# A recurrent attention, a dense MLP and a routed MLP on one core: the first gather of rows issued ahead of weight loads, more identity matmuls on TensorE, small routing results in PSUM

## The chip, the core and the metric

The kernel runs on one core of one Trainium2 chip. The metric is device time in microseconds, from one execution to the next the same program on the same data. The engines are named as the profile names them: PE is TensorE's matmul and PEld its weight load, DVE is VectorE, ACT is ScalarE, POOL is GpSimd, SP is SyncE, whose queue issues most of the DMAs. PE, DVE, ACT, POOL and SP each take their own instructions in the order of the program and wait on semaphores for one another.

## What is computed

Three stages follow each other, all in float32. The attention is a linear recurrence over 768 steps for 4 x 8 heads of size 48; its output is laid out as 3072 tokens of 384. A dense MLP with a leaky activation follows, then a gate with 8 columns, and a greedy assignment that takes the logits in falling order and fills each of 8 experts with exactly 384 tokens. Each expert is a two-layer MLP on its own tokens.

```python
for t in range(S):                                   # S = 768, per batch and head
    y[:, :, t] = rt . (state + u*kt (x) vt)
    state = w * state + kt (x) vt
h = x @ w_in; x = (max(h, 0) + alpha * min(h, 0)) @ w_out   # 3072 x 384 -> 2048 -> 384
for idx in argsort(-logits.flatten()):               # logits = x @ w_gate, 3072 x 8
    if assigned[tok] >= 0 or counts[e] >= cap: continue     # cap = 384
    assigned[tok] = e; counts[e] += 1
out[mask] = max(x[mask] @ w1[e], 0) @ w2[e]          # w1: 384 x 1024, w2: 1024 x 384
```

## The kernel before

**Setup and attention.** The recurrence is done in 24 chunks of 128 steps (4 batches by 6). `att_setup` builds powers of w by doubling on DVE and POOL (`PW`, `IW`, `TK`, `TR`), issues the first loads of k, r and v on SP, and prepares the first two chunks. Per chunk, `scale_k` multiplies k by powers of w (on POOL unless an engine is handed over), `turn_k` transposes the product on PE, `keep_k` copies the transposed tile to SBUF on ACT (`KT`), `scale_r` scales r on DVE (`RT`), `product` multiplies `RT` by `KT` (`prod`, on POOL unless handed over), and `sums` multiplies `prod` by `uw` on PE with two columns at a time, where `uw` is u times w. `keep_sums` copies the result (`cs`) on DVE. `scores` (`pA`) and the rest of `turn(i)` follow. In line 271, `warm(n)` issues n matmuls of the identity with itself on PE, whose result nobody reads; one appears in the trace as two instructions. The list `WARM` holds how many stand at each place of the setup: 8, 8 and 4, and a fourth entry that nothing uses. Beside the chunks, float64 words of the MLP's weights are taken apart on DVE (lines 481 to 488, `ti` and `tf`) and split into a high and a low part on ACT and POOL (lines 491, 492).

**Dense MLP.** Seven groups of tokens run with PE as the busy engine; every factor is split into a high and a low float32r part, so each product is three matmuls. The rows are written to `md` in DRAM by SP (line 650). In the last group the second layer is put off (`rest`), and its matmuls are spread over the steps of the first routing.

**Routing.** `route(p)` picks the tokens of the p-th expert to be filled. `close(p)` narrows a threshold in four passes: DVE compares (`G`, line 839), PE counts with six matmuls against one-hot rows `ohr` (`cnt`, line 844), and DVE transposes, sums and updates (`tr`, `tot`, `Je`, `jt`, `fl`, lines 848 to 859). After the fourth pass DVE finds the expert number (`F`, `Jm`, `sel`, `es`, `ei`, lines 861 to 874) and the members (`memb`). `lists` and `compact` turn members into row numbers (`px`, `ip`, `iw`, `idx`). `next_picks` and `next_ones` take the members out and prepare the keys and the one-hot rows (`eq`, `S`, `ohr`, which ACT copies three times, line 767) of the next pass. `tot` and the second `jt` are tiles in SBUF; `S` is one PSUM tile in which most other small results of the routing lie.

**First routing and first gather.** `first_route` runs `route(0)` beside `rest`. As soon as `ei` is known, `wload` issues the first expert's weights on SP: eight pieces of 384 KB into eight `raw` buffers, w1 in pieces 0 to 3 and w2 in 4 to 7. The first four go out at once; with `PRE` = 1 one of them is split in the same stretch (`wsplit`: a cast on ACT, line 1135, and a subtraction on POOL, line 1136). The other four wait, since POOL writes one element of each of their buffers (line 1125), and that stands behind the gather in POOL's queue. The last tile of the dense MLP is copied by ACT (line 649) and written to `md` by SP (line 650), behind the first four loads. `gather` then issues three indirect DMAs on POOL (line 1142), 128 rows each.

**Experts.** The string `START` sets the order of the work around the gather, a letter each: `d` takes the remaining loads, `c` is one step of the second routing, `t` transposes one of the three gathered tiles on PE (line 1156), `l` makes its low part on DVE (`fxl`), `w` splits one weight piece. `PLAN0` places the splits that are left. In the loop, `layer1` (line 1172, `eph`) and `layer2` (line 1189, `o`) of expert p share PE with one step of the routing of the next expert each (`step`), so that routing p+1 runs beside expert p.

Of the kernel before, what the change touches and what calls it, by code (L numbers as in the profile page):

```python
# [8 lines left out]
F32 = mybir.dt.float32  # L9
# [3 lines left out]
U32 = mybir.dt.uint32  # L13
# [5 lines left out]
P = 128  # L19
B, H, S, D = 4, 8, 768, 48  # L20
# [16 lines left out]
NP = 8  # L37
# [3 lines left out]
START = "dcccwtwltclwtlc"  # L41
# [3 lines left out]
WARM = (8, 8, 4, 4)  # L45
PRE = 1
BASE = 6
EXTRA = ()
PLAN0 = ((0, 0), (0, 1), (1, 0), (1, 1))
# [36 lines left out]
class Kernel:  # L86
# [29 lines left out]
    def route_consts(self):  # L116
# [31 lines left out]
        self.iot, self.jt = S[:, 168:192], S[:, 192:224]  # L148
# [5 lines left out]
    def att_setup(self, ctx):  # L154
# [41 lines left out]
        for i in range(8):  # L196
            if i < 7:
                v.reciprocal(IW[:, i, :], PW[:, i, :])
                v.tensor_mul(PW[:, i + 1, :], PW[:, i, :], PW[:, i, :])
            if i == 0:  # L200
                g.tensor_copy(TR[:, :, 127], IW[:, 0, :])
            else:
                i -= 1
                n = 1 << i
                pb = PW[:, i, :].unsqueeze(2).to_broadcast([112, 4, n])
                ib = IW[:, i, :].unsqueeze(2).to_broadcast([112, 4, n])
                v.tensor_mul(TK[:, :, P - 2 * n:P - n], TK[:, :, P - n:], pb)
                g.tensor_mul(TR[:, :, P - 2 * n:P - n], TR[:, :, P - n:], ib)
        TKm = ap.tile([P, 4, P], F32, name="TKm")
# [16 lines left out]
        for q in range(2):  # L226
            o = slice(64 * q, 64 * q + D)
            v.tensor_mul(self.uw[o, :, q], uc[o], PW[o, 0, :])
        self.keep_k(0)
        self.product(0, v)  # L230
        self.turn_k(1, tag="y", bufs=2)
        self.keep_k(1)
        self.sums(self.prod.pop(0))
        self.keep_sums(0)
        self.scale_k(2)
# [374 lines left out]
    def mlp(self, ctx):  # L610
# [41 lines left out]
        for gi, T in enumerate(GROUPS):  # L652
# [22 lines left out]
            for f in range(NF):  # L675
                if (gi, f) == (late - 2, 12):
                    self.route_consts()
                if gi == 0 and f == 8:
                    nc.sync.dma_start(self.wgb, bass.AP(tensor=self.w_gate.tensor, offset=self.w_gate.offset,
                                                        ap=[[0, P], [1, DM * E]]).rearrange("p (e c) -> p e c", e=E))  # L680
# [145 lines left out]
    def close(self, p):  # L826
# [5 lines left out]
        for s in range(STEPS):  # L832
# [16 lines left out]
            tot = rp.tile([P, E], F32, name="tot")  # L849
# [15 lines left out]
        jt = rp.tile([P, 32], F32, name="jt")  # L865
# [245 lines left out]
    def wload(self, ei, s, behind=False):  # L1111
# [4 lines left out]
        for c in range(NP):  # L1116
            raw = (self.rw if c < NP // 2 else self.rw2).tile([P, 2 * DM], F32, name="raw")
            if c < NP // 2:
# [4 lines left out]
            else:  # L1123
                if behind:
                    nc.gpsimd.memset(raw[:1, :1], 0.0)
# [7 lines left out]
    def wsplit(self, piece):  # L1133
        d, to = piece
        self.nc.scalar.copy(to[0], d)  # L1135
        self.nc.gpsimd.tensor_sub(to[1], d, to[0].bitcast(F32))  # L1136

# [81 lines left out]
    def route(self, p):  # L1219
# [7 lines left out]
        yield from cut(ls, 2 if p else 99)  # L1227
        if p < E - 1:
            self.next_picks(p)
        if p > 1:  # L1230
            yield
        yield from ls
        self.idxs[p] = self.idx
        if p < E - 1:
            self.next_ones(p)

    def first_route(self, rest):
# [4 lines left out]
        for n, _ in enumerate(self.route(0)):  # L1242
            if load is None and self.eis:
                load = self.load = self.wload(self.eis.pop(0), 0, True)
                self.pieces = [next(load) for _ in range(NP // 2)]
            elif len(self.pieces) > NP // 2 - PRE and n > 10:
                self.wsplit(self.pieces.pop(0))
            drain(cut(rest, REST[n]))

    def experts(self):  # L1250
# [18 lines left out]
        for c in START:  # L1269
# [8 lines left out]
            elif c == "w":  # L1278
                self.wsplit(self.pieces.pop(0))
            else:  # L1280
                self.pieces.extend(self.load)
# [121 lines left out]
```

## Time and profile before

| | us |
|---|---|
| median of 3 runs | 802.99 |
| lowest and highest run | 801.01, 804.59 |
| the profiled execution | 804.11 |
| its span from first to last instruction | 802.3 |
| PE busy in it | 769.6 |
| DVE busy in it | 589.3 |
| ACT busy in it | 409.6 |
| POOL busy in it | 279.5 |

A row of a timeline gives the start in microseconds from the span's start, the duration, engine, source line, operation, output and inputs, shapes and how many instructions were merged; the bracket at the end tells how long the engine stood idle before and what released it. [...] Times of the sections below are positions in this profiled execution.

### The profile page before, as it was taken

How to read it: one execution, taken by the hardware profiler on the slowest of the kernel's cores; microseconds unless marked ns; L12 is line 12 of the kernel's file. 1: busy time of each engine (PE TensorE's matmuls, PEld its weight loads, DVE VectorE, ACT ScalarE, POOL GpSimd, SP SyncE). 2: the span in 40 equal slices, each digit the busy share in tenths (PEclk: the TensorE clock that was granted, in tenths of full speed). 3: DMA queues.
4: the chain of work that ended last, by engine and by line, in shares of the span. 5: the costliest groups of instructions: out<-in, count | busy, mean ns of one | idle time of the engine just before them, and what ended most of it. 6: DMA issues, size and time to landing. Idle time of an engine off the chain costs nothing.

```text
span 802.3 us, 15416 instructions
## 1 busy us (share of the span) xinstructions
PE 769.6 (96%) x5539; PEld 706.0 (88%) x5539; DVE 589.3 (73%) x1601; ACT 409.6 (51%) x884; POOL 279.5 (35%) x273
## 2 busy tenths in 40 slices
PE   7999999999999999999999999995999999999996
PEld 6888987989999899999998999884889989889996
DVE  6899996997899999888885444776777778664220
ACT  3889896665444444534444455714335444344441
POOL 6788872322000000000000000006667766658661
PEclk8799999999999999999999999996999999999998
DMA  8688873620100200301020010014542553554300
GB/s 236 187 244 241 262 227 91 211 85 24 56 1 0 80 1 3 106 20 31 24 76 0 1 60 1 21 53 155 187 155 81 199 177 96 162 159 148 129 31 32
DMA packets 64579, 81.30 MB, mean 101 GB/s; under 512 B 8048, under 2 KB 55408, under 8 KB 64368
## 3 DMA queue, kind: packets, MB, share of 16 engines
q1 hardware_dynamic: 61008, 70.81, 28.5%
q0 software_dynamic: 3072, 9.44, 3.5%
q8 instruction: 45, 0.74, 0.4%
q14 instruction: 38, 0.31, 0.1%
q10 hardware_dynamic: 416, 0.00, 0.0%
HBM read 66.07 MB, written 14.16 MB: 100 GB/s over the span
## 4 chain that ended last, share of the span: by engine, by line
PE 69%; DVE 7%; issue 3%; ACT 2%; POOL 1%; DMA 1%; POOLq 0%; SPq 0%; another core or an unknown queue 0%; ACTq 0%; DVEq 0%
PE m L638 25%; PE ph L691 24%; PE eph L1172 9%; PE o L1189 9%; PE cnt L844 1%; DVE G L839 1%; PE ept L1156 1%; DVE gh L706 1%; POOL wbl L1136 1%; POOL out_dram L1198 1%; DVE fxl L1162 1%; ACT nt L695 1%; PE ip L949 1%; DMA xg<-md,idx 0%; DVE F L861 0%
## 5 line engine op out<-in xcount | busy, mean ns | idle before, releaser
L691 PE MATMUL ph<-xh,wah 128*128 128x512 f32 (+1 forms) x336 | 121.8, 363 | 1.0 <-ACTq L244 0.7
L691 PE MATMUL ph<-xh,wal 128*128 128x512 f32 (+1 forms) x336 | 121.5, 362 | 0.0
L691 PE MATMUL ph<-xl,wah 128*128 128x512 f32 (+1 forms) x336 | 121.5, 362 | 0.0
L695 ACT ACTIVATE nt<-ph 128x512 f32<-128x512 f32 (+1 forms) x112 | 60.2, 538 | 118.1 <-PE ph L691 112.1
L638 PE MATMUL m<-wbh,gl 128*128 128x384 f32 (+1 forms) x352 | 119.2, 339 | 0.4 <-DVE gl L717 0.4
L638 PE MATMUL m<-wbh,gh 128*128 128x384 f32 (+1 forms) x352 | 119.2, 339 | 0.0
L638 PE MATMUL m<-wbl,gh 128*128 128x384 f32 (+1 forms) x352 | 119.1, 338 | 0.0
L706 DVE SCALAR_TENSOR_TENSOR gt<-nt,al,gt 128x512 f32<-128x512 f32 (+1 forms) x96 | 67.8, 706 | 49.6 <-ACT gt L696 49.6
L714 ACT CAST gh<-gt 128x512 fp32r<-128x512 f32 (+1 forms) x96 | 56.3, 587 | 72.9 <-DVE gt L706 72.9
L1175 ACT ACTIVATE hh<-eph 128x384 fp32r<-128x384 f32 x64 | 31.5, 492 | 117.1 <-PE eph L1172 110.2
L134 POOL MEMSET io<- 128x1 f32 x1 | 0.1, 100 | 252.5 <-DVE io L133 252.5
L1180 DVE SCALAR_TENSOR_TENSOR hl<-eph,hh 128x384 fp32r<-128x384 f32 x64 | 35.5, 555 | 64.0 <-ACT hh L1175 57.6
L562 DVE SCALAR_TENSOR_TENSOR junk<-wt,wgb 128x384 f32<-128x384 f32 x128 | 71.3, 557 | 3.9
L691 PEld LDWEIGHTS ph<-xh,wal 128*128 128x128 f32 x336 | 63.1, 188 | 10.6
L691 PEld LDWEIGHTS ph<-xh,wah 128*128 128x128 f32 x336 | 63.1, 188 | 9.1 <-ACTq L244 1.0
L717 DVE TENSOR_TENSOR gl<-gt,gh 128x512 fp32r<-128x512 f32 (+1 forms) x96 | 61.8, 643 | 12.7 <-ACT gh L714 12.6
L1136 POOL TENSOR_TENSOR wbl<-raw,wbh 128x768 fp32r<-128x768 f32 x32 | 58.7, 1853 | 31.7 <-ACT wbh L1135 31.6
L691 PEld LDWEIGHTS ph<-xl,wah 128*128 128x128 f32 x336 | 63.1, 188 | 7.3
L1136 POOL TENSOR_TENSOR wal<-raw,wah 128x768 fp32r<-128x768 f32 x32 | 58.6, 1851 | 30.7 <-ACT wah L1135 27.9
L638 PEld LDWEIGHTS m<-wbh,gh 128*128 128x128 f32 x352 | 66.1, 188 | 3.4
L638 PEld LDWEIGHTS m<-wbl,gh 128*128 128x128 f32 x352 | 66.1, 188 | 3.3
L638 PEld LDWEIGHTS m<-wbh,gl 128*128 128x128 f32 x352 | 66.1, 188 | 0.7 <-DVE gl L717 0.7
(263 smaller groups left out, 1798.7 us busy)
## 6 DMA issues: line engine op xcount, KB each, us to landing
raw<-in_moe_w_dram SPq DMA_DIRECT2D x64, 384.0 KB
raw<-in_moe_w_in_dram SPq DMA_DIRECT2D x16, 384.0 KB
raw<-in_moe_w_out_dram SPq DMA_DIRECT2D x16, 384.0 KB
raw_r<-in_rt_dram SPq DMA_DIRECT2D x24, 224.0 KB
raw_k<-in_kc_dram SPq DMA_DIRECT2D x24, 192.0 KB
raw_v<-in_vc_dram SPq DMA_DIRECT2D x24, 192.0 KB
xd<-ysb SPq DMA_DIRECT2D x48, 96.0 KB
md<-raw SPq DMA_DIRECT2D x22, 192.0 KB
```

The lines of the kernel that those rows point to most:

```text
L562: v.scalar_tensor_tensor(junk, t, 1.0, self.wgb[:, e], op0=ALU.mult, op1=ALU.mult, accum_out=wc[:, f, e:e + 1])
L638: nc.tensor.matmul(acc[t][:, :N], a[:, o], self.wb[b][:, f, :N], start=(f == 0 and n == 0), stop=(f == NF - 1 and n == 2))
L691: nc.tensor.matmul(ph[:, :T], self.wa[a][:, k, fs], b[:, k, :T], start=(n == 0), stop=(n == 8))
L695: nc.scalar.activation(nt[:, :T], ph[:, :T], AF.Relu, scale=-1.0)
L706: v.scalar_tensor_tensor(gt[:, :T], nt[:, :T], self.al[:, f:f + 1], gt[:, :T], op0=ALU.mult, op1=ALU.add)
L714: nc.scalar.copy(h, g)
L717: v.tensor_sub(l, g, h.bitcast(F32))
L1136: self.nc.gpsimd.tensor_sub(to[1], d, to[0].bitcast(F32))
L1172: self.nc.tensor.matmul(ph, w1[a][:, k, f * P:(f + 1) * P], x[b][:, k], start=(n == 0), stop=(n == 8))
L1175: self.nc.scalar.activation(hh, ph, AF.Relu)
L1180: self.nc.vector.scalar_tensor_tensor(hl, ph, 0.0, hh.bitcast(F32), op0=ALU.max, op1=ALU.subtract)
L1189: self.nc.tensor.matmul(self.acc[q], h[a][:, o], w2[b][:, f], start=(f == 0 and n == 0), stop=(f == NS - 1 and n == 2))
```

## The change

Constants: `WARM` goes from (8, 8, 4, 4) to (8, 8, 10, 6), and its fourth entry is now used, between the transposes of the first two chunks and `sums`. `PRE` goes from 1 to 2. `START` and `PLAN0` are new; a digit n in `START` issues n identity matmuls, `s` does only the subtraction of a piece that was cast before.

```diff
-START = "dcccwtwltclwtlc"
+START = "dssc996ctc6tl6tlclc"
-WARM = (8, 8, 4, 4)
-PRE = 1
+WARM = (8, 8, 10, 6)
+PRE = 2
-PLAN0 = ((0, 0), (0, 1), (1, 0), (1, 1))
+PLAN0 = ((0, 0), (0, 1), (1, 0), (1, 1), (2, 0), (2, 1))
@@ att_setup
+        for q in range(2):                       # behind the loop that builds TR
+            o = slice(64 * q, 64 * q + D)
+            g.tensor_mul(self.uw[o, :, q], uc[o], PW[o, 0, :])
         self.scale_r(1)
-        for q in range(2):
-            o = slice(64 * q, 64 * q + D)
-            v.tensor_mul(self.uw[o, :, q], uc[o], PW[o, 0, :])
         self.keep_k(0)
         self.product(0, v)
+        self.scale_k(2, v)
         self.turn_k(1, tag="y", bufs=2)
         self.keep_k(1)
+        self.warm(WARM[3])
         self.sums(self.prod.pop(0))
         self.keep_sums(0)
-        self.scale_k(2)
         self.product(1)
@@ mlp, last group, f == 6
+                    i0 = self.rp.tile([2, 1], U32, name="i0")
+                    nc.gpsimd.memset(i0, 0)
+                    nc.gpsimd.indirect_dma_start(
+                        out=self.rp.tile([2, DM], F32, name="r0"), out_offset=None, in_=self.md[:P, :],
+                        in_offset=bass.IndirectOffsetOnAxis(ap=i0, axis=0))
@@ route_consts and close
-        self.iot, self.jt = S[:, 168:192], S[:, 192:224]
+        self.iot, self.jt, self.jt2, self.tot = S[:, 168:192], S[:, 192:224], S[:, 224:256], S[:, 256:264]
-            tot = rp.tile([P, E], F32, name="tot")
+            tot = self.tot
-        jt = rp.tile([P, 32], F32, name="jt")
+        jt = self.jt2
@@ wload: pieces in a given order; only the piece number `held` is written by POOL first
-        for c in range(NP):
+        for n, c in enumerate(order):
+            if n == held:
+                nc.gpsimd.memset(raw[:1, :1], 0.0)
-                if behind:
-                    nc.gpsimd.memset(raw[:1, :1], 0.0)
@@ first_route
-                load = self.load = self.wload(self.eis.pop(0), 0, True)
-                self.pieces = [next(load) for _ in range(NP // 2)]
-            elif len(self.pieces) > NP // 2 - PRE and n > 10:
-                self.wsplit(self.pieces.pop(0))
+                load = self.load = self.wload(self.eis.pop(0), 0, ORDER, PRE)
+                self.pieces = [next(load) for _ in range(PRE)]
+            elif 11 < n < 12 + PRE:
+                self.wcast(self.pieces[n - 12])
@@ route(p), p > 0: next_ones one step earlier
         if p > 1:
             yield
+        if p:
+            next(ls)
+        if p < E - 1:
+            self.next_ones(p)
+        if p:
+            yield
         yield from ls
-        if p < E - 1:
-            self.next_ones(p)
```

Two weight pieces now go out ahead of the gather instead of four, in the order 0, 1, 4, 2, 5, 3, 6, 7 (`ORDER`), and the third holds the five behind it on SP. Both early pieces are cast on ACT after the copy of the dense MLP's last tile, and their subtractions on POOL stand behind the gather.

On PE the setup reads as follows; `pt` and `pk` are transposes, `kvc` on the `uw` row is `sums`. Before:

```order
L212 MATMUL pt<-ident,TK 128x112 x4
L271 MATMUL warm<-ident 128x128 x4
L364 MATMUL pk<-ident,raw_p_116 112x128 x4
L364 MATMUL pk<-ident,raw_p_118 112x128 x4
L336 MATMUL kvc<-uw,prod 64x2 x8
```

Now:

```order
L215 MATMUL pt<-ident,TK 128x112 x4
L272 MATMUL warm<-ident 128x128 x10
L365 MATMUL pk<-ident,raw_p_116 112x128 x4
L365 MATMUL pk<-ident,raw_p_118 112x128 x4
L272 MATMUL warm<-ident 128x128 x6
L337 MATMUL kvc<-uw,prod 64x2 x8
```

Six more identity matmuls stand ahead of the first transposes, and six new ones between the transposes and the first `sums`.

On POOL, around the first gather (`xg` are the three gathered tiles, `wal` low parts of weights, `raw` the one-element write that lets later loads start, `r` the new small gather of two rows). Before:

```order
L141 MEMSET F 128x32
L796 COPY L<-M 128x176
L796 COPY L<-M 128x16
L1136 TENSOR_TENSOR wal<-raw,wah 128x3x256
L1142 DMA xg_6929<-md,idx 128x384
L1142 DMA xg_6931<-md,idx 128x384
L1142 DMA xg_6933<-md,idx 128x384
L1125 MEMSET raw 1x1 x4
```

Now:

```order
L141 MEMSET F 128x32
L681 MEMSET i_6421 2x1
L682 DMA r_6423<-md,i_6421 2x384
L803 COPY L<-M 128x176
L803 COPY L<-M 128x16
L1156 DMA xg_6937<-md,idx 128x384
L1156 DMA xg_6939<-md,idx 128x384
L1156 DMA xg_6941<-md,idx 128x384
L1126 MEMSET raw 1x1
L1146 TENSOR_TENSOR wal<-raw,wah 128x3x256 x2
```

The subtraction has moved behind the gather, and a small indirect DMA from `md` stands ahead of it, in the last group of the MLP.

On PE behind the first routing's last matmul (`iw`), where `o` are the transposes of the gathered tiles. Before:

```order
L957 MATMUL iw<-is__6880,two 32x6 x4
L844 LDWEIGHTS ohr_5665
L844 MATMUL cnt<-G,ohr_5665 128x128
...
L1156 MATMUL o_6971<-ident,xg_6929 128x128 x3
L1156 MATMUL o_6979<-ident,xg_6931 128x128 x3
```

Now:

```order
L964 MATMUL iw<-is__6887,two 32x6 x4
L272 MATMUL eph<-ident 128x128 x24
L851 LDWEIGHTS ohr_5678
L851 MATMUL cnt<-G,ohr_5678 128x128
...
L1170 MATMUL o_6994<-ident,xg_6937 128x128 x3
L272 MATMUL eph<-ident 128x128 x6
L1170 MATMUL o_7018<-ident,xg_6939 128x128 x3
L272 MATMUL eph<-ident 128x128 x6
L1170 MATMUL o_7031<-ident,xg_6941 128x128 x3
```

The 24 identity matmuls stand ahead of the second routing's first count and of the first gathered tile; the third transpose has moved ahead of the second count.

## Rows read from the trace of the kernel before

**Rows 1.** The granted clock in the page's 40 equal slices (20 us each), in tenths.

```profile
PEclk8799999999999999999999999996999999999998
```

**Rows 2.** Stretches: length; busy PE, PEld, DVE, ACT, POOL (instructions); PEclk, DMA share, GB/s.

```profile
16.00:29.00 13.00, 13.00 (x152) 11.33 (x152) 8.59 (x20) 9.52 (x27) 8.10 (x8) 0.50 0.79 214
30.00:43.00 13.00, 12.45 (x222) 10.81 (x218) 12.56 (x28) 12.06 (x36) 10.22 (x11) 1.00 0.71 176
```

**Rows 3.** Timeline of the setup: identity matmuls, uw, the two products, sums.

```profile
1.68 3.68 PE L271 MATMUL warm<-ident 128*128 128x128 f32 x16 [1.68 <-DVE ident L110]
...
8.17 1.07 PE L271 MATMUL warm<-ident 128*128 128x128 f32 x8
...
10.91 1.01 DVE L228 TENSOR_TENSOR uw<-uc,PW 48x4 f32<-48x4 f32 x2
...
11.87 1.26 POOL L376 TENSOR_TENSOR prod<-RT,KT 112x512 f32<-112x512 f32 x1 [0.15 <-ACT KT L370]
11.95 1.73 DVE L376 TENSOR_TENSOR prod<-RT,KT 112x512 f32<-112x512 f32 x1
...
13.73 0.63 PE L336 MATMUL kvc<-uw,prod 112*64 112x2 f32 x16 [2.62 <-DVE prod L376]
```

**Rows 4.** The chain that ended last, around the first gather: start, us, what.

```profile
537.71 3.25 DMA raw<-in_moe_w_dram
540.98 0.83 ACT wah L1135
541.81 0.39 ACT gt L649
542.21 2.77 DMA md<-gt
...
545.37 0.63 issue
...
546.22 3.88 DMA xg<-md,idx
550.15 0.92 PE o L1156 x3
...
553.85 3.26 PE eph L1172 x9
...
560.70 0.52 PE cnt L844 x6
```

**Rows 5.** Timeline of POOL and PE around the first gather.

```profile
542.56 0.24 PE L957 MATMUL iw<-is__6880,two 64*32 64x6 f32 x8 [0.55 <-DVE is__6880 L954]
...
546.22 1.15 POOL L1142 DMA_INDIRECT xg<-md,idx  x1 [2.52 <-DVE ohr L764]
...
546.51 0.80 PE L844 MATMUL cnt<-G,ohr 128*128 128x128 bf16 x6 [3.71 <-DVE G L839]
...
547.68 0.97 POOL L1142 DMA_INDIRECT xg<-md,idx  x1 [0.30 <-issue]
```

**Rows 6.** Timelines of later routings: F alone and beside POOL's subtraction, and PE's waits.

```profile
588.48 0.17 DVE L861 TENSOR_SCALAR F<-tot 128x8 f32<-128x8 f32 x1
...
645.55 5.44 POOL L1136 TENSOR_TENSOR wbl<-raw,wbh 128x768 fp32r<-128x768 f32 x3 [2.77 <-ACT wbh L1135]
...
645.84 1.61 DVE L861 TENSOR_SCALAR F<-tot 128x8 f32<-128x8 f32 x1
...
648.41 0.23 DVE L868 TENSOR_SCALAR S<-jt,Jm 128x8 f32<-128x8 f32 x1
...
650.35 0.19 PE L922 MATMUL px<-memb,tri 128*128 128x24 bf16 x1 [1.38 <-DVE memb L884]
...
703.32 1.84 POOL L1136 TENSOR_TENSOR wbl<-raw,wbh 128x768 fp32r<-128x768 f32 x1 [0.78 <-ACT wbh L1135]
...
703.61 1.58 DVE L861 TENSOR_SCALAR F<-tot 128x8 f32<-128x8 f32 x1
...
707.37 0.55 PE L1156 MATMUL ept<-ident,xg 128*128 128x128 f32 x3 [1.89 <-DVE fxl L1162]
```

**Rows 7.** A stretch behind that last wait, columns as in rows 2.

```profile
708.30:711.60 3.30, 3.30 (x13) 2.99 (x12) 2.25 (x9) 1.59 (x3) 2.36 (x2) 0.50 0.83 239
```

**Rows 8.** Timeline of PE: the first count of a later routing.

```profile
690.21 0.50 PE L844 MATMUL cnt<-G,ohr 128*128 128x128 bf16 x6 [0.88 <-DVE G L839]
```

More of the change, by code (lines that the diff above doesn't have):

```diff
@@ L677, in mlp @@
                     self.route_consts()
+                if (gi, f) == (late, 6):
+                    i0 = self.rp.tile([2, 1], U32, name="i0")
[3 more added lines that the diff above has]
+                        in_offset=bass.IndirectOffsetOnAxis(ap=i0, axis=0))
                 if gi == 0 and f == 8:
@@ L1109, in wset, with wload @@
                 [t[:, 3 * F2:].rearrange("p (f c) -> p f c", c=DM) for t in (h, l)])
-    def wload(self, ei, s, behind=False):
+    def wload(self, ei, s, order=range(NP), held=None):
         nc = self.nc
@@ L1131, in wload, with wcast, wsub, wsplit @@
             yield d, to
-    def wsplit(self, piece):
+    def wcast(self, piece):
         d, to = piece
         self.nc.scalar.copy(to[0], d)
+    def wsub(self, piece):
+        d, to = piece
         self.nc.gpsimd.tensor_sub(to[1], d, to[0].bitcast(F32))
+    def wsplit(self, piece):
+        self.wcast(piece)
+        self.wsub(piece)
     def gather(self, idx):
@@ L1227, in route @@
         yield from cut(ls, 2 if p else 99)
+        if not p:
+            self.idxs[p] = self.idx
         if p < E - 1:
@@ L1277, in experts @@
                 self.warm(int(c), self.ph.tile([P, CAP], F32, name="eph")[:, :P])
-            elif c == "w":
-                self.wsplit(self.pieces.pop(0))
+            elif c == "s":
+                self.wsub(self.pieces.pop(0))
             else:
```

## Prediction, made before the changed kernel ran

> **What bounds the kernel now.** I read the page's slices first. PE is busy nearly everywhere, so the places that matter are those where it waits or runs slowly, and the granted clock names them: it is down in the first two slices, in one near 550 us and in the last [rows 1]. [...] The timeline shows what PE did before the clock fell: it stood idle for 2.62 us until DVE's product was there [rows 3]. Around the gather I read the chain that ended last. It runs from a weight load over a weight cast on ACT, the copy of the MLP's last tile, its write to DRAM, and the gather, to the first layer-1 block of expert 0 at 553.85 [rows 4]. Behind it PE is again the bound, but for a few waits, which the later routings cause [rows 6, 8].
>
> **Setup: the first product.** `uw` moves from DVE to POOL, whose place for it is idle time. On DVE its two small operations took 1.01 us, since POOL was at work on k then, and DVE's product took 1.73 us with POOL's at 1.26 beside it [rows 3]. Where POOL started first, such a DVE operation ends only after it. Now DVE's product can start as soon as `KT` is there, before POOL's second product, and take some 0.7 us. Against that stand the ten identity matmuls ahead of the transposes. At the lower level one instruction takes 3.68 / 16 = 0.23 us; half of that, 0.115, is the price at full clock, near the 1.07 / 8 = 0.13 of the later block [rows 3]. So the block of 20 instructions lasts 2.3 us from 8.17 and holds the transposes back by some 0.4 us. `scale_k(2)` now stands on DVE between the product and `cs`, next to POOL's product, for 0.9 to 1.6 us. I take a gain of 0.4 us for all of this, out of 0 to 1.0 (the stretch in which DVE's product was held).
>
> **Setup: the clock.** The identity matmuls fill most of PE's gap: 2.3 us and then 12 x 0.115 = 1.4 us behind the transposes, so the idle time ahead of `sums` falls from 2.62 us to under 1. If the clock then stays up, DVE's idle time from 16 to 29, 13 - 8.59 = 4.4 us, falls towards the 13 - 12.56 = 0.4 of the later stretch [rows 2]. That is 4.0 us at the most. I take 3.4, since the first chunks have fewer matmuls to hide waits. The time carries through, as DVE works through its list in order until the dense MLP starts. If the clock falls as before, the gain is 0. Setup together: -3.8 us, from -0.4 to -5.0.
>
> [...] Between 8.2 and 11 us PE did identity matmuls and transposes in about equal parts, and the clock held until after the idle stretch. [...]
>
> **First gather.** Four things shorten the chain [rows 4]. The cast on ACT (0.83 us) no longer stands ahead of the tile's copy, which waits for PE's last matmul instead: about 0.5 us earlier. The tile's write follows two weight loads instead of four and should land in some 2.0 us instead of 2.77: 0.8. The stretch marked "issue" ahead of the first gather (0.63 with its neighbours, 1.24 from the landing at 544.98 to 546.22) is not there ahead of the second one, which comes 0.30 us after the first; and the first takes 1.15 us against 0.97 [rows 5]. The small gather in the MLP takes that first-use cost, if it is one: some 1.1. Together 2.4 us.
>
> Now the block of 24 identity matmuls decides. PE ends `iw` at 542.8 [rows 5]; 48 x 0.115 = 5.5 us bring it to 548.3, the count's 0.5 to 548.8, where the first tile (546.22 - 2.4 + 3.7 = 547.5) has landed. Three transposes of 0.35 with two blocks of 1.4 between them and the second count follow: layer 1 starts near 553.1 instead of 553.85, 0.7 us earlier. At full clock its first block takes half of 3.26 us, which is 1.6 more. But the second routing's counts stand between the layer-1 blocks on PE, and its first count is now at 548.3 instead of 546.51 [rows 5]. So the count at 560.70 [rows 4] cannot gain the full 2.3; I take the middle, -1.4 us, from 0 to -2.4. The weight loads held behind the gather start near 547.6 (543.8 and three gathers of 0.97 and 0.30); casts and subtractions keep their order behind them, and before PE waited for none of them here.
>
> **Small results in PSUM.** `F` takes 0.17 us alone, but 1.61 and 1.58 us where POOL's subtraction runs; `sel`, which writes PSUM, takes 0.23 in the middle of one [rows 6]. `F` reads and writes SBUF; with `tot` in PSUM I expect it at its 0.2. That takes 1.4 us from each of the two chains, and PE waits at their ends: 1.38 us for `memb` and 1.89 for the low part of a tile [rows 6]. PE has no other wait there, so both gains count: -2.8. Behind the second wait the clock is at 0.50 for 3.3 us, with PE busy throughout [rows 7], which cost 1.65 us; with a wait of 0.5 it probably stays up. I count half of it: -0.8. Together -3.6, from -1.4 to -4.5. The reductions into PSUM may cost up to the difference of `sel` and `F` alone, 0.06 us each, beside PE work: nothing.
>
> **next_ones earlier.** Three DVE operations and ACT's copies leave the stretch between `idx` and the next `G`. PE's wait there is 0.88 us [rows 8]; elsewhere it is short. -0.9, from 0 to -0.9.
>
> **Sum.** -3.8 - 1.4 - 3.6 - 0.9 = -9.7 us from the profiled execution, 804.11 us, gives 794.4. That execution is 1.1 us above the median of the three runs, 802.99, so I forecast 793.3.
>
> **Rivals.** First, the clock falls in the setup all the same, because the first chunks have few matmuls with many columns. For it speaks that the trace held it at 0.50 for 13 us with PE busy all the time [rows 2]; against it, that the 2.62 us gap came first and that later chunks hold it. The setup then gives 0.4: -6.3, 796.7 us. [...]
>
> Second, the gather gives nothing: the 1.24 us are no first-use cost, so the small gather doesn't do what it is for, and PE's block covers the rest. -8.3, 794.7 us.
>
> Third, `F` is still held by POOL, because it still writes SBUF. The PSUM part gives 0: -6.1, 796.9 us.
>
> Fourth, slower: identity matmuls do not lift the clock. Then each costs 0.23 us per instruction. The gather block lasts 11 us, to 553.8, and the two behind it 2.8 each; layer 1 starts near 563 instead of 553.85, 9 us late, and the setup loses some 4 through 20 + 12 such instructions. With -4.5 from the routings that is +8.5, or 811.5. It decides once an instruction of the block takes over (550.15 - 542.8) / 48 = 0.15 us. Against it: the first block ran at 0.23 and the third at 0.13 [rows 3], with little but such matmuls between.
>
> **How the numbers follow.** The forecast 0.60, the first rival 0.18, the second 0.08, the third 0.05, two of these three together (799 to 801) 0.05, the fourth 0.04. The range takes all bounds on the good side (-5.0 - 2.4 - 4.5 - 0.9 = -12.8, 790.2) and on the bad side the first and third rival with some of the rest short: 790 to 800. About 0.5%, 4 us, is what a measurement tells from no change. Under 799 lie the forecast and most of the first three rivals, 0.86; within 4 us the pairs and the weak ends, 0.10; above, 0.04.
>
> **What would show it.** Right: granted clock 1.00 from 11 us on, DVE busy for over 11 of 13 us from 16 to 29; the gather on POOL near 544; layer 1 before 553.5 and at full clock; no `F` over 0.3 us; no wait of PE over 1 us between 575 and 710. Wrong: clock 0.50 anywhere from 12 to 29, a gather still at 545 or later, PE in identity matmuls when the tile has long landed, or a new wait on a weight subtraction on POOL in expert 0.

## The result, and the profile after

The changed kernel takes **794.33 us** (median of 9 runs, 793.72 to 795.06). Beside it, the kernel before took 802.99 (9 runs, 797.67 to 806.93). The ratio is 0.990, with a 95% interval of 0.9876 to 0.9924: faster by about 8.7 us. The forecast was 793.3, in a range of 790 to 800.

The profiled execution of the changed kernel took 793.72 us, with a span of 791.7. It lies 10.4 us below the profiled execution of before, which was itself 1.1 above its median, while this one is 0.6 below. The rows below are compared between these two executions, so they add up to 10.6, the difference of the spans, and not to 8.7.

The granted clock in the page's 40 slices (as rows 1; PEclk is the granted TensorE clock as a share of full speed), one of the two stretches of the setup (as rows 2) and the timeline of the setup (as rows 3):

```profile
PEclk9999999999999999999999999999999999999998
```

```profile
16.00:29.00 13.00, 11.35 (x199) 9.06 (x196) 11.42 (x25) 12.51 (x37) 10.32 (x10) 1.00 0.94 254
```

```profile
8.10 0.47 POOL L211 TENSOR_TENSOR uw<-uc,PW 48x4 f32<-48x4 f32 x2
8.16 2.41 PE L272 MATMUL warm<-ident 128*128 128x128 f32 x20
...
9.02 1.89 POOL L350 TENSOR_TENSOR raw_p<-raw_k,TKm 128x384 f32<-128x384 f32 x1 [0.46 <-POOL uw L211]
9.50 0.55 DVE L350 TENSOR_TENSOR raw_p<-raw_k,TKm 128x384 f32<-128x384 f32 x1
...
10.96 1.09 PE L365 MATMUL pk<-ident,raw_p 128*112 128x128 f32 x8 [0.40 <-POOL raw_p L350]
...
12.27 0.69 DVE L377 TENSOR_TENSOR prod<-RT,KT 112x512 f32<-112x512 f32 x1 [1.62 <-ACT KT L371]
...
13.32 0.63 PE L337 MATMUL kvc<-uw,prod 112*64 112x2 f32 x16
```

The clock stays at 1.00 from 16 to 29 us, where it was 0.50, and DVE is now busy for 11.42 of the 13 us instead of 8.59 [rows 2]. The first sums start 0.4 us earlier than in rows 3, although the first transposes start 0.9 us later (10.96 against 10.03): the scaling of k on POOL, whose result they wait for, took 1.89 us instead of 1.00.

Around the first gather (as rows 4 and 5; PE, POOL and SP's write):

```profile
538.68 0.34 SPq L651 DMA_DIRECT2D md<-gt  x1
...
539.56 0.24 PE L964 MATMUL iw<-is__6887,two 64*32 64x6 f32 x8 [0.54 <-DVE is__6887 L961]
...
539.74 5.62 PE L272 MATMUL eph<-ident 128*128 128x128 f32 x48
...
542.35 1.01 POOL L1156 DMA_INDIRECT xg<-md,idx  x1 [21.09 <-DVE S L910]
...
545.20 0.50 PE L851 MATMUL cnt<-G,ohr 128*128 128x128 bf16 x6
...
545.53 0.50 PE L1170 MATMUL o<-ident,xg 128*128 128x128 f32 x3
...
549.93 0.79 PE L1186 MATMUL eph<-fxh,wah 128*128 128x384 f32 x3 [0.23 <-ACT fxh L1172]
```

PE goes from the 24 identity matmuls (the block) into the count and the tile's transposes without a bracket: nothing is late when the block ends, so the block sets the time there. `G` was ready at 543.4, 1.8 us before the count.

`F` in all routings, and one of them beside POOL (as rows 6):

```profile
L868 DVE TENSOR_SCALAR F<-S x7: 166/166/167, 532.1 to 696.9; 128x8 f32<-128x8 f32 x7
```

```profile
640.80 3.67 POOL L1146 TENSOR_TENSOR wbl<-raw,wbh 128x768 fp32r<-128x768 f32 x2 [2.78 <-ACT wbh L1142]
641.10 0.17 DVE L868 TENSOR_SCALAR F<-S 128x8 f32<-128x8 f32 x1
```

PE's waits from 537 us on (what it waited for; us in total, times, longest), and the count that answers to rows 8:

```profile
PE cnt L851 <- DVE G L846: 2.9, 4, 1.2
PE px L929 <- DVE memb L891: 0.8, 2, 0.5
PE iw L964 <- DVE is__7272 L961: 0.6, 1, 0.6
...
PE ept L1170 <- DVE fxl L1176: 0.5, 1, 0.5
```

```profile
683.49 0.49 PE L851 MATMUL cnt<-G,ohr 128*128 128x128 bf16 x6 [0.17 <-issue]
```

The wait of 1.38 us for `memb` in the fifth routing and the one of 1.89 for the low part of a tile have gone or shrunk to 0.5 [rows 6], and the 0.88 for `G` [rows 8] is 0.17. The clock behind the tile is now 1.00, where it was 0.50 [rows 7]:

```profile
700.00:704.00 4.00, 4.00 (x26) 3.85 (x26) 3.72 (x13) 2.65 (x6) 2.87 (x2) 1.00 0.81 252
```

One wait is new: 0.6 us for `iw` of the second routing.

Where the time went, by the start of the same instruction in both traces:

| instruction | before | after | difference |
|---|---|---|---|
| first `gt` of the dense MLP on DVE | 130.34 | 126.59 | -3.75 |
| `px`, first routing | 538.20 | 535.21 | -2.99 |
| `iw`, first routing | 542.56 | 539.56 | -3.00 |
| `px`, second routing | 565.00 | 560.38 | -4.62 |
| `iw`, second routing | 570.77 | 566.86 | -3.91 |
| `px`, fourth routing | 620.32 | 615.97 | -4.35 |
| `px`, fifth routing | 650.35 | 644.19 | -6.16 |
| `iw`, sixth routing | 685.74 | 679.71 | -6.03 |
| first count behind it | 690.21 | 683.49 | -6.72 |
| `iw`, seventh routing | 718.12 | 708.41 | -9.71 |
| `iw`, eighth routing | 728.84 | 719.02 | -9.82 |
| end of the last matmul | 794.72 | 784.10 | -10.62 |

Two differences of it were not foreseen: the dense MLP, from the first `gt` to the first `px`, gives back 0.76 us, and the stretch behind the last `iw` gains 0.8.

### The profile page after: what moved, and what is told of

The parts are those of the page before. It is cut to its first block, busy times and chain, and to the rows that moved or that the text cites. A ratio compares the mean times of both kernels' runs of the same rounds, so it can differ in the third digit from the quotient of the medians.

```text
span 791.7 us, 15609 instructions
## 1 busy us (share of the span) xinstructions
PE 769.7 (97%) x5635; PEld 706.0 (89%) x5635; DVE 584.6 (74%) x1600; ACT 409.7 (52%) x884; POOL 280.3 (35%) x273
## 4 chain that ended last, share of the span: by engine, by line
PE 69%; DVE 8%; issue 3%; ACT 2%; POOL 1%; POOLq 0%; ACTq 0%; DVEq 0%
PE m L639 25%; PE ph L698 23%; PE o L1203 9%; PE eph L1186 8%; DVE G L846 1%; PE cnt L851 1%; PE eph L272 1%; PE ept L1170 1%; DVE gh L713 1%; POOL out_dram L1212 1%; DVE fxl L1176 1%; POOL wbl L1146 1%; ACT nt L702 1%; DVE hl L1194 1%; DVE tr L855 0%
```

## Experiments

Times are medians. The kernel before ran beside all of them, with medians of 801.8 to 802.9. The versions of the changed kernel scatter little (the changed kernel itself lies between 793.1 and 795.1 in 19 runs), so they are compared with one another directly, and finer things by positions in their traces. The changed kernel ran again beside some of them; that run is called the yardstick.

### The setup: identity matmuls away, and identity matmuls alone

```diff
 # first run: changed kernel
-WARM = (8, 8, 10, 6)
+WARM = (8, 8, 4, 0)
 # second run: kernel before
-WARM = (8, 8, 4, 4)
+WARM = (8, 8, 10, 6)
         self.keep_k(1)
+        self.warm(WARM[3])
         self.sums(self.prod.pop(0))
```

> The changed kernel with the identity matmuls of the setup at their old number: 4 instead of 10 ahead of the first transposes, none instead of 6 behind the second ones; uw, the products and scale_k(2) stay as changed. Clock theory (the prediction's): PE again stands idle for 1.2 to 1.5 us ahead of the first sums, the granted clock falls to 0.50 behind it for some 13 us, and the time is 3 to 3.5 us above the changed kernel, near 797.6. Rival (the shorter DVE product alone closed the gap enough): the clock stays at 1.00 and the time is within 0.4 us of the changed kernel, near 794.4. In both, the first transposes still start near 10.9 us, as they wait for POOL's scaled k there and not for identity matmuls.

> The kernel before with nothing changed but the identity matmuls of the setup: 10 ahead of the first transposes, 6 more behind the second ones. Clock theory: they alone keep the clock at 1.00 from 12 to 29 us; DVE is busy for over 11 of the 13 us from 16 to 29, and the time is 2.8 to 3.6 us below the kernel before (799.4 to 800.2 by the median of 803.0). Rival (uw on POOL and the early product are needed too, since DVE's product still ends at 13.7): PE is idle for 0.7 us or more ahead of the sums, the clock falls, and the time is within 0.5 us of the kernel before.

Without them the changed kernel takes 797.12 us (794.26 to 798.89, 8 runs), some 3 us more than with them. Its profiled execution, 794.76 us, is one of its faster ones. A stretch of the setup there, columns as in rows 2:

```profile
16.00:29.00 13.00, 13.00 (x174) 11.21 (x173) 10.19 (x23) 10.30 (x31) 9.19 (x9) 0.64 0.83 226
```

The clock falls again, and PE is busy throughout. PE had been idle for 1.73 us ahead of the transposes and 0.97 ahead of the sums. The clock theory holds; the rival is out.

The kernel before with the identity matmuls alone takes 799.4 us (10 runs), a ratio of 0.9975 (0.9952 to 0.9997): 2.4 us less than the 801.83 beside it, a little short of the 2.8 to 3.6 expected. In its trace the clock holds with nothing else changed (the stretch as in rows 2), and the setup shows more than was expected:

```profile
16.00:29.00 13.00, 11.57 (x191) 9.27 (x192) 12.45 (x27) 11.92 (x36) 10.12 (x10) 1.00 0.91 250
```

```profile
10.41 1.04 PE L365 MATMUL pk<-ident,raw_p 128*112 128x128 f32 x8
...
11.66 0.69 DVE L377 TENSOR_TENSOR prod<-RT,KT 112x512 f32<-112x512 f32 x1 [0.19 <-ACT KT L371]
...
12.71 0.63 PE L337 MATMUL kvc<-uw,prod 112*64 112x2 f32 x16
```

DVE's product is alone here too, at 0.69 us and without `uw` having been moved, because the identity matmuls hold the transposes back by 0.4 us and DVE is done with `uw` by then. The first sums start at 12.71, not at the 13.32 of the changed kernel, and the dense MLP's first `gt` at 125.75 instead of 126.59. So the moves in the setup cost about 0.6 us at the first sums, and the gain there is the identity matmuls' own.

### The first gather: no identity matmuls, fewer of them, no small gather

```diff
 # first run
-START = "dssc996ctc6tl6tlclc"
+START = "dsscctctltlclc"
 # second run
-START = "dssc996ctc6tl6tlclc"
+START = "dssc96cc6t6tlc6tlcl"
 # third run: the indirect DMA of two rows in the MLP and its index are taken out
```

> The changed kernel without the identity matmuls around the first gather (36 of them, 24 ahead of the first count and 6 behind each of the first two gathered tiles). Theory: with the 24 in place PE reaches the first count at 545.2 though G has been ready since 543.4, so the count now starts 1.8 us earlier; PE then waits for the first gathered tile, and that wait shows when it lands. If the clock falls for lack of PE work, 0.50 in 541 to 557, layer 1 runs at half speed and the time is 1 to 3 us above the changed kernel. Rival: between 550 and 567 DVE's chain of counts is what PE waits for (3.4 us in all), so the early count is worth more than the clock, and the time is 0.5 to 1.8 us below the changed kernel.

> The changed kernel with 15 instead of 24 identity matmuls ahead of the first count, 6 behind the count, 6 behind the first and 6 behind the second tile, and the second count ahead of the third tile instead of behind it. Theory: the first count starts at 543.4 (1.8 us earlier), the second near 546.7 instead of 549.2, the fourth near 553.7 instead of 556.1; the clock stays at 1.00 and layer 1 still starts near 549.9; PE's waits for G and memb (2.8 us between 552 and 561) go, and the time is 1.5 to 2.5 us below the changed kernel. Rival: the clock falls between the pieces, layer 1 runs at half speed and the time is 1 us or more above. Second rival: the waits go, but the later wait for is_ of expert 1 grows by as much, and the time is within 0.5 us.

> The changed kernel without the small gather in the MLP. First-use theory (the prediction's): the first large gather pays it, starts 0.9 to 1.1 us later on POOL behind the landing of the last tile's write and takes 1.15 instead of 1.01 us; the first gathered tile lands near 546.5 instead of by 545.5, PE waits about 1 us for it, and layer 1 starts 0.5 to 1.1 us later against iw. Of that 0 to 1.1 us reach the end, since the counts' chain on DVE has waits of its own behind it (expected 0.4). Rival (no such cost): the first gather starts as in the changed kernel, and nothing in the trace behind it differs by over 0.2 us.

Without identity matmuls the kernel takes 793.57 us, and with the short block 793.52 (4 runs each); the changed kernel takes 794.33 in the first comparison and 793.8 as the yardstick (10 runs, on another chip). Both are 0.2 to 0.8 us faster, so the short block's 1.5 to 2.5 did not come, and the first run is nearest its rival. Without identity matmuls, the wait for the first tile becomes visible, and the clock is at half speed (PE, then a stretch with columns as in rows 2):

```profile
546.17 0.90 PE L1170 MATMUL o<-ident,xg 128*128 128x128 f32 x3 [1.22 <-DMA xg<-md,idx]
```

```profile
541.00:550.00 9.00, 3.96 (x21) 2.78 (x21) 6.21 (x18) 2.87 (x5) 6.43 (x6) 0.52 0.44 132
```

From `iw` of the first routing to `iw` of the second it needs 26.84 us, the changed kernel 27.30. So the clock is lost here, the first count comes earlier, and in sum nothing is lost: behind the gather DVE's chain of counts is late. With the short block, at full clock, the waits of PE show this directly:

```profile
543.63 0.49 PE L851 MATMUL cnt<-G,ohr 128*128 128x128 bf16 x6 [0.17 <-DVE G L846]
...
556.00 0.51 PE L851 MATMUL cnt<-G,ohr 128*128 128x128 bf16 x6 [1.65 <-DVE G L846]
```

Against `iw`, the first count starts 1.7 us earlier than in the changed kernel and the fourth only 0.25 earlier. The third count is over at 552.7, but the operations on its result stand on DVE behind the low part of layer 1's first block (`hl`), and DVE waits for that one until 552.94. The wait of 0.6 us for `iw` of the second routing is there as before (0.63). The second rival of that run is the nearest, with another cause than it named.

Without the small gather the time is 793.62 us (4 runs), the same. The first large gather:

```profile
542.49 1.15 POOL L1150 DMA_INDIRECT xg<-md,idx  x1 [20.72 <-DVE eq L903]
```

It takes 1.15 us instead of 1.01 and starts 2.42 us behind `iw`, where the two traces of the changed kernel have 2.79 and 2.33. There is a second part of a first-use cost. The write of the last tile and the gather behind it, in the kernel before with identity matmuls alone, which has no small gather, and in the combined version without identity matmuls at the gather, below, which has it (the chain that ended last):

```profile
537.51 3.82 DMA md<-gt
...
542.57 0.85 POOL xg L1143
```

```profile
538.03 2.19 DMA md<-gt
...
541.17 0.81 POOL xg L1156
```

From the landing of the write to the gather that is 1.24 us without the small gather and 0.95 with it. In all traces that show the landing it is 1.24, 1.24 and 1.15 without and 0.95 with it (seven traces). So the first-use cost is some 0.3 to 0.4 us in both parts together, not 1.1, and behind PE's block none of it reaches the time.

### The sum per expert back in SBUF

```diff
-            tot = self.tot
+            tot = rp.tile([P, E], F32, name="tot")
```

> The changed kernel itself, as the yardstick for the runs beside it on this chip. Both theories: 793.7 to 795.1 us, the span of its runs so far; granted clock 0.996 or more.

> The changed kernel with tot back in SBUF. Theory (the prediction's): F is held by POOL's subtraction again, for 1.6 us in two or more of the seven routings instead of 0.17; PE waits 1.2 to 1.4 us more for memb and for the low part of a tile behind them, the clock is at 0.50 for some 3 us behind one of these, and the time is 2.8 to 4.5 us above the changed kernel. Rival (the subtractions have moved against the routings with the earlier weight loads): F meets at most one, and the time is 0 to 1.4 us above. In both, jt of the routing, which stays in PSUM, has sel at 0.25.

The yardstick gives 793.8 us and this kernel 798.32 (10 runs each): 4.5 us. Timelines of the fifth and the seventh routing:

```profile
642.76 5.41 POOL L1146 TENSOR_TENSOR wbl<-raw,wbh 128x768 fp32r<-128x768 f32 x3 [2.77 <-ACT wbh L1142]
643.04 1.59 DVE L868 TENSOR_SCALAR F<-tot 128x8 f32<-128x8 f32 x1
...
647.56 0.19 PE L929 MATMUL px<-memb,tri 128*128 128x24 bf16 x1 [1.44 <-DVE memb L891]
...
699.81 1.59 DVE L868 TENSOR_SCALAR F<-tot 128x8 f32<-128x8 f32 x1
...
703.61 0.55 PE L1170 MATMUL ept<-ident,xg 128*128 128x128 f32 x3 [1.92 <-DVE fxl L1176]
```

`F` ends as the first of POOL's three subtractions ends (642.76 + 5.41 / 3 = 644.56). A third `F`, in the second routing, takes 1.33 us here, which in the kernel before took 0.25, as the subtractions now run at that place. From the first `iw` to the end of the last matmul this kernel needs 3.9 us more than the yardstick (247.91 against 244.03; the first trace of the changed kernel has 244.54); by the gaps between the `iw`, 1.15, 1.39 and 1.40 belong to the three. The rest of the 4.5 lies ahead of the first `iw`, where these kernels vary by as much from run to run.

One expectation failed. PE waits 1.92 us for the tile, as in rows 6, but the clock holds:

```profile
703.00:706.00 3.00, 2.39 (x16) 2.24 (x17) 2.86 (x11) 1.81 (x3) 0.52 (x1) 1.00 0.32 91
```

The kernel before with identity matmuls alone, whose routings are those of the kernel before, shows the same: the wait is there, and the clock holds.

```profile
702.53 0.55 PE L1157 MATMUL ept<-ident,xg 128*128 128x128 f32 x3 [1.89 <-DVE fxl L1163]
```

```profile
703.00:706.00 3.00, 3.00 (x20) 2.84 (x19) 2.73 (x11) 1.95 (x3) 1.59 (x1) 1.00 0.70 223
```

So the half-speed stretch of rows 7 is not the price of that wait alone.

### next_ones of the second routing at its old place

```diff
-        if p < E - 1:
+        if p != 1 and p < E - 1:
             self.next_ones(p)
...
         self.idxs[p] = self.idx
+        if p == 1:
+            self.next_ones(p)
```

> The changed kernel with next_ones of the second routing (expert 1) at its old place behind the lists; the other routings stay as changed. Theory: in that routing the early next_ones (M, S, eq, S, ohr on DVE, about 1.5 us with what lies between) stands ahead of is_, so PE waits 0.6 us for iw; with it late that wait goes and the next count, which had no wait in the kernel before, still has none: 0.6 us below the changed kernel. Rival: the wait only moves to the count's G behind it, and the time is within 0.3 us of the changed kernel.

The time is 793.39 us (4 runs), 0.4 below the yardstick, which is within the scatter of either. From the first `iw` to the second it is 0.70 faster (26.59 against 27.29 and 27.30 in the two traces of the changed kernel). The new wait is gone, and the count behind has almost none:

```profile
567.64 0.24 PE L964 MATMUL iw<-is__7267,two 64*32 64x6 f32 x8
571.37 0.49 PE L851 MATMUL cnt<-G,ohr 128*128 128x128 bf16 x6 [0.15 <-DVE G L846]
```

So the move costs 0.6 to 0.7 us in this routing: on DVE, its three operations (`eq`, `S`, `ohr`) stand ahead of `is_`, which PE's `iw` waits for.

### Versions built from these findings

The first undoes the moves in the setup and keeps its identity matmuls. The other three also have `next_ones` of the second routing late, and differ at the gather: no identity matmuls; the short block with one more count ahead of layer 1; the short block.

```diff
 # all four, att_setup
-        for q in range(2):                       # behind the loop that builds TR
-            o = slice(64 * q, 64 * q + D)
-            g.tensor_mul(self.uw[o, :, q], uc[o], PW[o, 0, :])
...
         self.scale_r(1)
+        for q in range(2):
+            o = slice(64 * q, 64 * q + D)
+            v.tensor_mul(self.uw[o, :, q], uc[o], PW[o, 0, :])
         self.keep_k(0)
         self.product(0, v)
-        self.scale_k(2, v)
...
         self.keep_sums(0)
+        self.scale_k(2)
 # third version only
+START = "dssc96cc6t6tlc6tlclc"
             l1 = self.layer1(f, x[p][0], w[0])
-            step()
+            if j:
+                step()
```

> The changed kernel with the setup's moves undone (uw back on DVE ahead of the product, scale_k(2) back on POOL behind the sums), its identity matmuls kept. Theory from the run of the kernel before with identity matmuls: the moves themselves cost time, since POOL's two uw operations let DVE's scaling of k get ahead and hold POOL's, so that the first transposes start at 10.96 instead of 10.41; undone, the first sums start at 12.7 instead of 13.3, the dense MLP 0.8 us earlier (125.8 instead of 126.6), and the time is 0.6 to 0.9 us below the changed kernel (near 793.1). Rival (the prediction's): the moves are worth 0.4 us, and the time is 0.4 us above.

> Three edits together: the setup's moves undone, next_ones of expert 1 late, and no identity matmuls around the first gather. If they add up as their traces showed (0.8, 0.6 and 0.5 us), the time is 1.9 us below the changed kernel, near 791.9; the clock is at 0.52 from 541 to 550. Rival (the lower clock costs something once the other waits are gone): 792.4 or more, and above the version with the short block beside it.

> The setup's moves undone, next_ones of expert 1 late, 15 identity matmuls ahead of the first count, 6 behind it and behind the first two tiles, and the third count of the second routing ahead of layer 1 instead of behind its first block (one step of the routing taken before layer 1 starts, and one less behind it). Theory: the third count starts near iw + 10.4 instead of + 12.5, the fourth no longer waits 1.65 us for G, and PE's waits between 550 and 567 fall from 3.4 to under 2 us: 2.5 to 3 us below the changed kernel, near 791.1. Rival: layer 1 starts 0.5 us later behind that count and the chain waits elsewhere: near 792.3, as the version with the short block.

> The setup's moves undone, next_ones of expert 1 late, and the short block around the gather (15, 6, 6, 6 identity matmuls; second count ahead of the third tile). If the gains add up (0.8, 0.6 and 0.25 us): 1.7 us below the changed kernel, near 792.1, with the clock at 1.00 throughout 541 to 560. Rival (keeping the clock up is worth more here than without these edits): 0.3 us or more below the version without identity matmuls beside it.

| version | median, us | runs | ratio to before (95%) |
|---|---|---|---|
| setup's moves undone | 793.78 | 792.88 to 794.44 | 0.9885 (0.9869 to 0.9902) |
| + `next_ones` late, no identity at the gather | 792.11 | 791.80 to 792.67 | 0.9870 (0.9854 to 0.9887) |
| + `next_ones` late, count ahead of layer 1 | 793.50 | 792.95 to 798.35 | 0.9905 (0.9873 to 0.9938) |
| + `next_ones` late, short block | 792.11 | 791.80 to 793.55 | 0.9867 (0.9850 to 0.9883) |

Undoing the moves alone does not show in the time (793.78 against 793.80 of the yardstick, on another chip, where 793.1 was expected), though in its trace the first sums start at 12.71 instead of 13.34; its profiled execution loses that again by the dense MLP (first `gt` at 127.44). The 0.6 us are shown by the first sums (12.71 or 12.72 in five traces without the moves, 13.32 to 13.34 in seven with them and all identity matmuls), and not by this time: by the first `gt` the two groups overlap, 125.75 to 127.44 against 126.59 to 128.08. Two of the combined versions, at 792.1 (791.9 and 792.1 expected), beat both kernels: the four runs of the one without identity matmuls at the gather, 791.8 to 792.7, lie below all 19 of the changed kernel. The two are equal, so the identity matmuls at the gather are worth nothing in this kernel, with the clock at 0.56 without them:

```profile
541.00:550.00 9.00, 5.75 (x26) 4.45 (x27) 6.56 (x21) 2.11 (x4) 6.57 (x6) 0.56 0.62 178
```

The count ahead of layer 1 failed: the third count comes at `iw` + 11.45 instead of the 12.80 of the short block beside it, but the fourth at 17.21 instead of 16.58, as on DVE the operations in between still stand behind `hl` of layer 1's first block, which now starts later. PE waits 2.06 us for `G` ahead of that fourth count, and `iw` of the second routing is 0.65 later than with the short block.

## Why the prediction was right, and where its steps were wrong

**The total** was 1.0 us too low, well inside the range. The mechanisms of the setup's clock and of the results in PSUM carried it. The smaller steps were wrong in both directions, and that they nearly cancel is luck. One reason is common to several: the sum was read from a single execution of the kernel before, and not all that it shows comes again. From the sixth `iw` to the seventh it takes 32.38 us; the kernel before with identity matmuls, whose code there is the same, takes 30.08, and the changed kernel 28.70.

**Setup, forecast -3.8, measured -3.75** at the first `gt` of the dense MLP. That the two agree so closely is luck: in seven traces of kernels with this setup that `gt` lies between 126.59 and 128.08, which is 2.3 to 3.75 us ahead of the one trace of before. The clock term was -3.4. By the medians the identity matmuls alone gain 2.4 us, and taking them away costs some 3; in the traces they gain 4.6 by this position (130.34 to 125.75, the shorter product included), but that sets the fastest execution of the one kernel against one of the other that is above its median.

The term for the moves was a gain of 0.4, and they cost 0.6. The step that failed is "DVE's product can start as soon as `KT` is there": it does, but `KT` is 0.9 us later than before, where the sum allowed 0.4 for the identity block. The rest is POOL's scaling of k, which was held by DVE's from 9.50 on (1.89 us instead of 1.00). I had counted `uw` on POOL as idle time and priced only the identity block ahead of the transposes. Which of the two scalings goes first hangs on little: in all six traces with `uw` on DVE, POOL's starts 0.53 to 0.54 us ahead of DVE's, takes 1.00 us, and DVE's is held (0.88 to 0.89); in all eight with `uw` on POOL it starts 0.12 to 0.48 ahead, and DVE's runs in 0.55 while POOL's is held (1.54 to 1.89). What decides it was not tried.

**The first rival**, a clock that falls in the setup all the same, is out: it stays at 1.00 from 16 to 29 us, with the transposes and short matmuls of the chunks and none of the added identity matmuls in that stretch. The transposes (`pk`) are only 12 of the 199 instructions of PE in that stretch, 1.9 of its 11.35 us, so what the clock does under transposes alone is not shown.

**First gather, forecast -1.4, measured -1.6** at `px` of the second routing (from one `px` to the next 25.17 us, 26.80 before, and 27.42 before with identity matmuls alone). Against `iw` the gather started 0.9 us earlier (1.3 in the yardstick) and not 2.4. Of the four pieces, the write's issue came 0.5 us earlier against `iw` (0.88 ahead of it instead of 0.35), as forecast. From its issue to the gather it takes 3.67 us (3.22 in the yardstick) instead of 4.01, a gain of 0.3 to 0.8, where 0.8 was forecast for the write and most of 1.1 for the first use. The write landed after 1.9 to 2.7 us with two loads ahead of it (eight traces), near the forecast 2.0, against 2.77 and 3.82 with four; the first use was worth 0.3 to 0.4. The first tile is at PE 3.2 us after its gather starts (546.17 less 542.96 without identity matmuls, where PE waits for it) instead of 3.9; the sum took 3.7. Fewer loads in the queue could explain this, but the kernel before with identity matmuls alone, with four loads ahead, has 3.3, so the cause is open. No run puts the four loads or the early cast back, so these pieces are read from traces alone.

The block ended at 545.36, 5.8 us behind `iw`, as computed, and so the earlier tile did not decide. What I had not asked is whether keeping the clock up gains anything at this place. With these matmuls it doesn't, since DVE's chain is late behind the gather; without the block, the gain is 0.5 us larger.

**Small results in PSUM, forecast -3.6.** Both stalls of `F` went, 1.4 us each, as the run with `tot` in SBUF shows (1.39 and 1.40). Of the half-speed stretch I counted half, 0.8; it went wholly, an estimated 1.65, half of the 3.3 us at 0.50 [rows 7], but two kernels with `tot` in SBUF kept the wait and not the stretch. So no run shows that this term belongs to `F`; how often the stretch comes was not measured. By the medians `tot` is worth 4.5 us in the changed kernel, more than forecast, since without this part it would lose a third stall, 1.15 us, which the trace of before could not show: other weights' subtractions run at that routing now. In the traces `F` is held by POOL's subtraction: with `tot` in SBUF it ended with the subtraction, after 1.59 us, and with its input in PSUM it took 0.17 in the middle of one. "Where POOL started first, such a DVE operation ends only after it" is not what the scalings of k in the setup show: POOL's starts at 9.02 and takes 1.89 us, and DVE's, at 9.50, ends first, after 0.55. The third rival, that `F` is held because it still writes SBUF, fell with this.

**next_ones earlier, forecast -0.9.** At the place that I read, PE's wait fell from 0.88 to 0.17 us. But the kernel before with identity matmuls alone, where `next_ones` stands at its old place, has no wait there either:

```profile
685.39 0.49 PE L845 MATMUL cnt<-G,ohr 128*128 128x128 bf16 x6
```

So the 0.88 belonged to that one execution, and no run shows a gain of the move. In the second routing it put a wait of 0.64 ahead of `iw`. What it is worth in the other routings was not tried. I had asked only which wait the move takes away behind `idx`, and not who waits for what now stands behind the moved operations.

**Not forecast:** the dense MLP's 0.76 us loss and the last stretch's 0.8 us gain, told below. They cancel.

**The fourth rival**, identity matmuls that don't lift the clock, is out: the block ran at 5.62 / 48 = 0.117 us per instruction, at a granted clock of 1.00. That the setup's first block took 0.23 because of the lower level is not shown, since the profile shows no 0.50 there. What the traces show of 0.50 is layer 1's first block: one group of three matmuls starts 0.96 us behind the other in the kernel before (554.97 and 555.93, at 0.50), and 0.52 in the changed kernel (550.56 and 551.08, at 1.00).

## What to carry to other kernels

Keeping TensorE streaming paid here where TensorE's speed was what was waited for (the setup, 2.4 us by the medians where nothing else was changed), and gave nothing where another engine's chain was late (the gather, 792.11 us with the short block and without identity matmuls): before filling a gap, read what is late behind it. An operation that moves to another engine can change which of its neighbours there goes first and which is held (POOL's scaling of k, 1.89 us instead of 1.00), so price these and not only its own length. A small result that meets long operations of POOL is a candidate for PSUM (`F`, 0.17 us instead of 1.6), even where only some routings meet one now, since a shift elsewhere can bring others to it, as it did in the second routing (1.33 us in SBUF, 0.25 before). And a wait or a slow stretch read from one execution, as the 0.88 us [rows 8] and the 3.3 us at 0.50 [rows 7] were, is a forecast only if a second one shows it too.

## What the runs showed of the hardware that was not expected

**Matmuls at a granted clock of 1.00 do not always run at one pace.** In the dense MLP, where PE is busy throughout and its instructions are the same, the stretch from the first `gt` to the first `px` takes 407.86 us in the kernel before and 407.87 in its version with identity matmuls, but 408.62 in the changed kernel and 408.3 to 408.6 in the versions made from it. Behind the last `iw` it is the other way round: 65.88 and 65.91 us against 65.08 in the changed kernel and 64.9 to 65.3 in its versions. Layer 2 at the end of the kernel before, first and last of 25 matmuls in a row, and of 24 in the changed kernel:

```profile
790.14 0.34 PE L1189 MATMUL o<-wbh,hl 128*128 128x384 f32 x1
...
794.38 0.34 PE L1189 MATMUL o<-wbh,hl 128*128 128x384 f32 x1
```

```profile
779.79 0.33 PE L1203 MATMUL o<-wbh,hh 128*128 128x384 f32 x1
...
783.77 0.33 PE L1203 MATMUL o<-wbh,hl 128*128 128x384 f32 x1
```

That is 4.24 / 24 = 0.177 us from one to the next against 3.98 / 23 = 0.173, with the clock granted in full in both. All twelve traces of the changed kernel and its versions have the faster pace here, and the two of the kernel before and its version the slower one. So it follows the program and not the run; which part of the program it follows was not settled.

**A fall of the clock is not the same in every run.** Runs of the kernel before lie between 797.2 and 807.1 us, with mean granted clocks of 0.971 to 0.990, and the changed kernel without the setup's identity matmuls lies between 794.3 and 798.9 with 0.986 to 0.994. The changed kernel has 0.994 to 0.998 and stays within 2 us. So the change takes away most of the scatter, too. The setup's identity matmuls alone do not: the kernel before with them lies between 797.7 and 803.0, at 0.980 to 0.990.

**A first indirect DMA costs little extra here,** 0.14 us of its own (1.15 against 1.01) and 0.2 to 0.3 us between the landing of the write and its start (1.15 to 1.24 against 0.95).
